# Causal linear attention and an ELU feed-forward on one core: the state term moved to 64x64 array tiles, w_in loaded in halves, and a new opening order

## The chip, the core and the metric

The kernel runs on one core of a Trainium2 chip. A core has a matrix engine (TensorE, PE in the profile, with its weight loads as PEld), a vector engine (VectorE, DVE), an activation engine (ScalarE, ACT), a general engine (GpSimd, POOL) and a queue engine (SyncE, SP). The metric is the device time of one execution in microseconds (us); a time quoted for a kernel is the median of its runs.

## The reference

`q`, `k`, `v` are 4 batches x 8 heads x 768 positions x 64, float32. Attention is linear and causal with a decay `lam[h]` per head; in blocks,

```python
intra = (qb @ kb.T) * Dmask          # Dmask[i, j] = lam ** (i - j) for i >= j, else 0
out   = intra @ vb + (qb * lam ** (pos + 1)) @ kv_state
kv_state = lam ** block * kv_state + (kb * lam ** (block - 1 - pos)).T @ vb
```

The attention's output is laid out as `x` of 3072 tokens x 512 (8 heads of 64 side by side), and goes through a feed-forward: `h = x @ w_in` (512 x 2048), `g = h` where positive and `exp(h) - 1` elsewhere, `out = g @ w_out` (2048 x 512), float32.

## The kernel before

The work is cut into 24 chunks g of 128 positions. Chunk g is block g // 4 of batch g % 4, so four consecutive chunks are the four batches at one place of the sequence. All matrix work is in float16 with float32 sums. Chunks 0 to 3 are treated one by one, the others in pairs. `T`, `S`, `P`, `U`, `1` and `2` below are the letters by which the kernel's own list names the steps:

- `T` (L284) transposes q and k of a chunk on PE with an identity, for chunks 0 to 7. VectorE multiplies q^T by `qs`, the powers of lam, and ScalarE copies k^T. For chunks 8 and up SP does it with two transposing DMAs (L274, in the step `W`).
- `S` (L305) makes the scores. Two heads share the 128 rows of a transposed block, so each matmul has 64 rows; the two heads of a block of rows go to two PSUM banks. VectorE multiplies the scores by the mask (`pp`, L330).
- `P` (L339) makes x^T of a chunk in one bank: per pair of heads two matmuls with v (L350, 128 rows x 64 columns of the array), and from chunk 4 on two with the state (L356). There the state of a pair of heads is a 128x128 matrix whose off-diagonal 64x64 blocks are zero, zeroed once at the start by VectorE and ScalarE (`z`, `Z`), and half of it is the weights of a 128x64 matmul. One instruction per chunk takes the bank to SBUF as `xt`: for chunks 0 to 7 a copy on ScalarE or VectorE, after that a multiplication by `qs` on VectorE.
- `U` (L401) makes the chunk's contribution to the state, and VectorE adds it (L431), in two instructions of 64 rows, to the old state times lam^128, which POOL has made in two instructions of 64 rows (L390). POOL also makes `kd`, k times powers of lam (L192).
- `1:g:j` (L491) is the first GEMM for a quarter (a single chunk) or an eighth (a pair) of the 2048 columns, one PSUM bank of 512 values; a third number halves it. ScalarE takes the exponential and the positive part, VectorE combines them to `g` (L480). `2:g:j` (L532) is the second GEMM's part; after the last part ScalarE copies the result out and SP stores it.

The order on every engine is the order in which this program issues instructions; nothing is moved afterwards. `OPEN` (L52) lists the steps up to chunk 10's, written out by hand; behind it a loop (L643) adds the rest, in which a pair's scores are followed at once by a burst `B:` with the U and P steps of the previous pair. `w3` is three matmuls on zeros, which fill a wait on PE. `BANKS` (L67) gives PSUM banks to steps: A to D, M0, M1, and H, which has two buffers.

All of q, k, v, w_in and w_out come in by DMAs that POOL issues, with a cast to float16, in the order of `POOL_ORDER` (L47): `k0` is k of chunk 0, `i0` a slice of 256 columns of w_in, `o0` one of 256 rows of w_out, `d2` the product kd of chunk 2, `m4` the state product of chunk 4. Chunk 0's q alone is issued by SP (`raw_q`). These DMAs take eight semaphores in turn, so that each waits on POOL until the eighth before it has landed.

Of the kernel before, what the change touches and what calls it, by code (L numbers as in the profile page):

```python
# [14 lines left out]
def kernel(  # L15
# [23 lines left out]
    GPE = 8  # L39
# [8 lines left out]
        "k0 k1 q1 v0 q2 i1 k2 i0 v1 v2 i2 i3 o0 q3 k3 d2 d0 o1 i4 o2 i5 v3 o3 o5 o4 i6 i7 q4 o7 d1 o6 "  # L48
        "k4 m4 v4 k6 q6 v6 q10 m5 d4 k8 d5 d3 k10 d6 m6 q8 v10 d7 m7 v8"
# [18 lines left out]
        "S0=M0,D S1=A,C S2=B,C S3=D,B P0=M1 P1=M1 P2=M0 P3=D U0=M0 U1=D U2=B U3=M1 T0=B,A T1=B,M1 "  # L68
        "T2=B,M1 T3=A T4=B T5=D T6=A T7=M1 M2=C M3=M0 H0_2=A H3_0=B X2=1 H0_1=C H1_3=A X3=1 X7=1 X4=1 "
        "H2_1=D X0=1 H1_1=M0"  # L70
# [26 lines left out]
    for i in range(7):  # L97
# [23 lines left out]
        [cpool.tile([128, NHP, 128], FP16, name=f"st{b}_{i}") for i in range(2)]  # L121
# [49 lines left out]
    def emit_wi(i):  # L171
        f0 = sum(WI[:i]) * 128
        nc.gpsimd.dma_start(  # L173
            out=wi16[i][:],
            in_=moe_w_in[:, f0 : f0 + WI[i] * 128].rearrange("(k p) f -> p k f", p=128),
        )
# [37 lines left out]
    def zero_st1(b):  # L214
        nc.vector.memset(st[b][1][:], 0.0)


# [8 lines left out]
    qs = cpool.tile([128, NHP, 128], FP32, name="qs")  # L226
    ks = cpool.tile([128, H], FP32, name="ks")
# [77 lines left out]
    def att_S(g):  # L305
        qt, kt = qkT[g]
        psS[g] = [
            bank(f"S{g}", hh, [128, NHP, 128], FP32, f"psS{g}_{hh}") for hh in range(2)
        ]
        for hp in range(NHP):  # L310
            for hh in range(2):
                r = slice(hh * 64, (hh + 1) * 64)
                nc.tensor.matmul(  # L313
                    psS[g][hh][:, hp, :], lhsT=kt[r, hp, :], rhs=qt[r, hp, :],
                    start=True, stop=True,
                )
# [21 lines left out]

    def att_P(g):  # L339
        cb, b = divmod(g, B)  # L340
        until(E_done, g)
        if cb > 0:
            until(Y_done, g - B)
        vt = of(vg, g)
        qt, _ = qkT[g]
        po = bank(f"P{g}", 0, [128, NHP, 128], FP32, f"psO{g}")
        R = [slice(0, 64), slice(64, 128)]
        for hp in range(NHP):
            for hh, r in enumerate(R):
                nc.tensor.matmul(  # L350
                    po[r, hp, :], lhsT=vt[:, 2 * hp + hh, :], rhs=Pt[(g, hh)][:, hp, :],
                    start=True, stop=(cb == 0), skip_group_check=True,
                )
            if cb > 0:
                for r in R:
                    nc.tensor.matmul(  # L356
                        po[r, hp, :], lhsT=st[b][cb % 2][:, hp, r], rhs=qt[:, hp, :],
                        start=False, stop=True, skip_group_check=True,
                    )

        def evacuate():
            g0 = GFIRST[g]
            n = GSIZE[g0]
            if g0 not in xg:
                xg[g0] = asb.tile(
                    [128, NHP, n * 128], FP16, tag=f"xt{n}", name=f"xt{g0}",
                    bufs=4 if n == 1 else 2,
                )
            dst = xg[g0][:, :, (g - g0) * 128 : (g - g0 + 1) * 128]
            if g < GPE:  # L370
                (nc.vector.tensor_copy if f"X{g}" in TAGS else nc.scalar.copy)(dst, po[:])
            else:
                nc.vector.tensor_tensor(out=dst, in0=po[:], in1=qs[:], op=ALU.mult)  # L373
            X_done.add(g)

        return [evacuate]

    stt = {}

    def att_M(g):  # L380
        cb, b = divmod(g, B)
        if cb == NCB - 1:
            return
        assert f"U{g - B}" in seen
        until(Y_done, g - B)
        old = st[b][cb % 2]
        for hh in range(2):
            r = slice(hh * 64, (hh + 1) * 64)
            tmp = asb.tile([128, NHP, 64], FP32, tag="stt", name=f"stt{g}_{hh}", bufs=8)
            nc.gpsimd.tensor_tensor(  # L390
                out=tmp[r], in0=old[r, :, r],
                in1=upp[r].unsqueeze(2).broadcast_to([64, NHP, 64]), op=ALU.mult,
            )
            stt[(g, hh)] = tmp
# [6 lines left out]
    def att_U(g, pu=None):  # L401

        cb, b = divmod(g, B)
        if cb == NCB - 1:
            return []
        vt = of(vg, g)
        if pu is None:
            full = bank(f"U{g}", 0, [128, NHP, 128], FP32, f"psU{g}")
            for hp in range(NHP):
                nc.tensor.matmul(  # L410
                    full[:, hp, :].rearrange("p (h e) -> p h e", h=2),
                    lhsT=kds[g][:, 2 * hp : 2 * hp + 2, :],
                    rhs=vt[:, 2 * hp : 2 * hp + 2, :], start=True, stop=True,
                )
        else:
            for hp in range(NHP):
                for hh in range(2):
                    r = slice(hh * 64, (hh + 1) * 64)
                    nc.tensor.matmul(  # L419
                        pu[r, hp, :], lhsT=kds[g][:, 2 * hp + hh, :], rhs=vt[:, 2 * hp + hh, :],  # L420
                        start=True, stop=True, skip_group_check=True,
                    )
        new = st[b][(cb + 1) % 2]

        def update(hh):
            r = slice(hh * 64, (hh + 1) * 64)
            src = full[r, :, r] if pu is None else pu[r, :, :]
            if cb == 0:
                nc.vector.tensor_copy(new[r, :, r], src)
            else:  # L430
                nc.vector.tensor_tensor(  # L431
                    out=new[r, :, r], in0=stt.pop((g, hh))[r], in1=src, op=ALU.add
                )
            if hh == 1:
                Y_done.add(g)

        return [lambda: update(0), lambda: update(1)]

    def burst(*ops):
# [3 lines left out]
        for o in ops:  # L443
            if o[0] == "P":
                evs += att_P(int(o[1:]))
# [130 lines left out]
    def zero_st(b):  # L576
        nc.scalar.memzero(st[b][0][:])

# [18 lines left out]
    def ready(t):  # L597

        g = int(t[1:])
        if t[0] == "P":  # L600
            assert g < B or f"U{g - B}" in seen
        if t[0] == "U" and g < 2 * B:
            assert "c2" in seen
            assert f"{'z' if g < B else 'Z'}{g % B}" in seen
# [4 lines left out]
    def run(t):  # L609
# [7 lines left out]
        if w in "PUzZ":  # L617
            ready(t)
        if w == "S":
            for g in a:  # L620
                att_S(g)
# [10 lines left out]
        else:  # L632
            {"T": att_T_pe, "1": mm1, "2": mm2, "Z": zero_st, "z": zero_st1,
             "q": lambda g, e: cast_raw(g, "q", e), "k": lambda g, e: cast_raw(g, "k", e),
             "c": const, "W": pool_work, "L": load_pair,
             "M": next_M, "w": zero_matmuls}[w](*a)
# [28 lines left out]
    for t in prog:  # L665
        run(t)
# [34 lines left out]
```

## Time and profile before

| | |
|---|---|
| median of 3 runs | 211.45 us (211.43 to 211.71) |
| profiled execution | 211.74 us, of which the instructions span 210.0 us |
| PE busy | 204.5 us, 97% of the span, 2075 matmuls |
| DVE, ACT, POOL busy | 137.3, 125.3 and 98.9 us |
| first GEMM (L511), second GEMM (L541) | 98.6 and 96.8 us of PE's busy time |
| matmuls with v (L350), with the state (L356) | 192 and 160 |
| granted PE clock | 1.00 |

The span runs from the first to the last instruction. Matmuls overlap in the array, so the busy time of a group is the time in which at least one of its matmuls was under way; the chain of waits, which gives each piece the time up to the next start, tells better what a group costs. Its columns are start in us, length in us, and the work.

### The profile page before, as it was taken

The numbers are of one execution on the slowest core, as the hardware profiler recorded it, in microseconds if no ns is written. First come the engines' busy times: TensorE is split into PE (matmuls) and PEld (weight loads), VectorE is DVE, ScalarE is ACT, GpSimd is POOL, SyncE is SP. The second block draws the span as 40 slices with busy tenths as digits, with TensorE's granted clock in tenths as the row PEclk, the third lists the DMA queues.
The fourth block names the chain that finished last, engine by engine and source line by source line (L and its number), as shares of the span: only waits on it lengthen the run. The fifth ranks groups of instructions, "written<-read, shape, count | busy, mean of one in ns | idle before, by whom it ended". The sixth has DMA issues, their size and how long they took to land.

```text
span 210.0 us, 5117 instructions
## 1 busy us (share of the span) xinstructions
PE 204.5 (97%) x2075; PEld 140.3 (67%) x2075; DVE 137.3 (65%) x238; ACT 125.3 (60%) x241; POOL 98.9 (47%) x113
## 2 busy tenths in 40 slices
PE   7899999999999999999999999999999999999994
PEld 3458767767777766767667667666666667666653
DVE  6778843699847879678686787676676763433320
ACT  2728565765675866586377377377377477577640
POOL 8999789699935948259294379100000000000000
PEclk9999999999999999999999999999999999999999
DMA  8999999999999999997999929993520110110112
GB/s 105 161 180 187 194 201 188 155 181 154 96 110 210 118 200 143 178 117 47 167 140 113 165 77 106 184 148 69 128 75 0 53 50 0 53 52 16 37 50 100
DMA packets 103079, 24.71 MB, mean 118 GB/s; under 512 B 93200, under 2 KB 100624, under 8 KB 103056
## 3 DMA queue, kind: packets, MB, share of 16 engines
q0 software_dynamic: 79760, 13.50, 85.0%
q1 hardware_dynamic: 22768, 10.76, 26.2%
q8 instruction: 16, 0.26, 0.5%
q10 hardware_dynamic: 528, 0.13, 0.3%
q14 instruction: 7, 0.06, 0.1%
HBM read 27.40 MB, written 6.29 MB: 160 GB/s over the span
## 4 chain that ended last, share of the span: by engine, by line
PE 80%; POOL 9%; DMA 9%; issue 1%; DVE 0%; POOLq 0%
PE psM L541 36%; PE psH L511 34%; DMA wo<-in_moe_w_out_dram 9%; PE psS L313 3%; PE psO L350 2%; PE psO L356 2%; POOL qn L133 2%; POOL wi L173 2%; POOL kn L133 2%; POOL kd L192 1%; POOL vn L133 1%; PE psU L419 1%; POOL wo L180 1%; PE psT L294 1%; PE psMrest L553 0%
## 5 line engine op out<-in xcount | busy, mean ns | idle before, releaser
L511 PE MATMUL psH<-xt,wi 128*128 128x256 f16 (+1 forms) x896 | 98.6, 257 | 0.1
L541 PE MATMUL psM<-wo,g 128*128 128x512 f16 (+1 forms) x384 | 96.8, 377 | 0.2
L520 ACT ACTIVATE e<-psH 128x512 f32<-128x512 f32 x96 | 57.4, 598 | 63.8 <-PE psH L511 63.4
L511 PEld LDWEIGHTS <-wi 128*128 128x128 f16 x896 | 78.0, 98 | 24.7
L480 DVE SCALAR_TENSOR_TENSOR g<-e,r 128x512 f16<-128x512 f32 x64 | 46.8, 732 | 40.6 <-ACT r L527 40.1
L541 PEld LDWEIGHTS <-g 128*128 128x128 f16 x384 | 35.8, 98 | 26.8 <-issue 0.4
L527 ACT ACTIVATE r<-psH 128x512 f32<-128x512 f32 x64 | 38.1, 595 | 0.0
L330 DVE TENSOR_TENSOR pp<-psS,mask 128x512 f16<-128x512 f32 x48 | 30.9, 684 | 1.9 <-PE psS L313 1.8
L480 DVE SCALAR_TENSOR_TENSOR g<-e,psH 128x512 f16<-128x512 f32 x32 | 21.9, 685 | 14.0 <-ACT psH L527 13.8
L192 POOL TENSOR_TENSOR kd<-kn,ks 128x512 f16<-128x512 f16 x20 | 21.5, 1081 | 16.7 <-DMA kn<-in_k_dram 15.9
L390 POOL TENSOR_TENSOR stt<-st,upp 64x256 f32<-64x256 f16 x32 | 21.6, 674 | 13.1 <-DVE st L431 11.7
L527 ACT ACTIVATE psH<-psH 128x512 f32<-128x512 f32 x32 | 19.1, 598 | 0.0
L567 ACT COPY osb<-psM 128x512 f32<-128x512 f32 (+1 forms) x24 | 14.1, 589 | 6.4 <-PE psM L541 6.4
L133 POOL DMA_DIRECT2D kn<-in_k_dram x14 | 15.5, 1111 | 1.3 <-POOLq L685 0.8
L133 POOL DMA_DIRECT2D vn<-in_v_dram x14 | 15.4, 1109 | 0.0
L133 POOL DMA_DIRECT2D qn<-in_q_dram x13 | 14.7, 1129 | 0.5 <-DMA wo<-in_moe_w_out_dram 0.5
L431 DVE TENSOR_TENSOR st<-stt,psU 64x256 f16<-64x256 f32 x32 | 13.3, 416 | 0.7
L350 PE MATMUL psO<-pp,vn 128*64 128x128 f16 x192 | 12.3, 221 | 0.3 <-ACT kT L302 0.2
L373 DVE TENSOR_TENSOR xt<-psO,qs 128x512 f16<-128x512 f32 x16 | 10.5, 685 | 2.4 <-PE psO L356 2.3
L350 PEld LDWEIGHTS <-vn 128*64 128x64 f16 x192 | 10.1, 109 | 2.8 <-issue 2.3
L88 PE MATMUL psZ<-zero 128*128 128x512 f16 x26 | 9.1, 514 | 1.2 <-DVE zero L83 1.2
L356 PE MATMUL psO<-qT,st 128*64 128x128 f16 x160 | 10.1, 219 | 0.0
(49 smaller groups left out, 91.6 us busy)
## 6 DMA issues: line engine op xcount, KB each, us to landing
out_dram<-osb SPq DMA_DIRECT2D x19, 256.0 KB, 3.6
qn<-in_q_dram POOLq DMA_DIRECT2D x10, 256.0 KB, 7.2
kn<-in_k_dram POOLq DMA_DIRECT2D x10, 256.0 KB, 9.3
vn<-in_v_dram POOLq DMA_DIRECT2D x10, 256.0 KB, 8.4
wi<-in_moe_w_in_dram POOLq DMA_DIRECT2D x8, 256.0 KB, 6.7
wo<-in_moe_w_out_dram POOLq DMA_DIRECT2D x8, 256.0 KB, 8.8
out_dram<-osb SPq DMA_DIRECT2D x8, 128.0 KB, 1.8
kn<-in_k_dram POOLq DMA_DIRECT2D x4, 128.0 KB, 5.1
```

Of the source, the lines that this page charges most:

```text
L133: nc.gpsimd.dma_start(out=t[:].rearrange("p b h d -> p (b h) d"), in_=src)
L192: nc.gpsimd.tensor_tensor(out=kd[:], in0=of(kg, g), in1=ks[:].unsqueeze(2).broadcast_to([128, H, 64]), op=ALU.mult,)
L330: nc.vector.tensor_tensor(out=P[:], in0=pts[hh][:], in1=mask[:, hh::2, :], op=ALU.mult)
L350: nc.tensor.matmul(po[r, hp, :], lhsT=vt[:, 2 * hp + hh, :], rhs=Pt[(g, hh)][:, hp, :], start=True, stop=(cb == 0), skip_group_check=True,)
L356: nc.tensor.matmul(po[r, hp, :], lhsT=st[b][cb % 2][:, hp, r], rhs=qt[:, hp, :], start=False, stop=True, skip_group_check=True,)
L390: nc.gpsimd.tensor_tensor(out=tmp[r], in0=old[r, :, r], in1=upp[r].unsqueeze(2).broadcast_to([64, NHP, 64]), op=ALU.mult,)
L480: nc.vector.scalar_tensor_tensor(out=flat, in0=e[:], scalar=-1.0, in1=r[:], op0=ALU.add, op1=ALU.min)
L511: nc.tensor.matmul(pH[:, f * n * 128 : (f + 1) * n * 128], lhsT=wi16[i][:, kk, w * 128 : (w + 1) * 128], rhs=xg[g0][:, kk, :], start=(kk = ...
L520: nc.scalar.activation(e[:], pH[:], AF.Exp)
L527: nc.scalar.activation(r[:], pH[:], AF.Relu)
L541: nc.tensor.matmul(psM[g][:, cols], lhsT=gts[(g, j * FB + f)], rhs=wo16[i][:, w, cols], start=mm2_done[g] == 1, stop=mm2_done[g] == NFT, s ...
L567: eng.copy(o[:], src)
```

## The change

Five things change together.

1. **x^T's rows.** A block of 128 rows of x^T now holds heads k and 4+k instead of 2k and 2k+1. The rows of w_in have to follow, so a slice of w_in is loaded by two transfers, each to 64 partitions: rows 0 to 255 of w_in and rows 256 to 511.
2. **The state term.** The state is kept as 64 columns per pair of heads, without the zero blocks, and its matmuls are 64 rows x 64 columns of the array. The two heads of a pair lie on different rows and write different banks, heads of the two halves lie on different columns; so four matmuls in a row use four different quarters of the array. A pair of chunks is done together (`att_PP`): the state term of both first, then the matmuls with v into the same two banks, each of which holds two blocks of rows for both chunks. Two instructions per pair take the banks out; from chunk 8 on VectorE multiplies by `qx`, the powers of lam in the new order of heads, which ScalarE makes at the step `x`. All evacuations of chunks 0 to 7 are on ScalarE.
3. **The state's update.** `U` of a single chunk is eight matmuls of 128x64 instead of four of 128x128 (as it was in the bursts already). VectorE's update and POOL's product are one instruction of 128 rows each instead of two of 64, and nothing is zeroed.
4. **Scores just ahead of a burst** (S14:15 to S22:23) are made in 64x64 tiles too, 32 matmuls instead of 16.
5. **Order.** `POOL_ORDER`, `OPEN` and `BANKS` are new: the opening transposes chunk 1 before chunk 0, makes the scores of both in a row, and starts the first GEMM after P1; chunks 8 to 11 come in another order.

```diff
-        "k0 k1 q1 v0 q2 i1 k2 i0 v1 v2 i2 i3 o0 q3 k3 d2 d0 o1 i4 o2 i5 v3 o3 o5 o4 i6 i7 q4 o7 d1 o6 "
-        "k4 m4 v4 k6 q6 v6 q10 m5 d4 k8 d5 d3 k10 d6 m6 q8 v10 d7 m7 v8"
+        "k0 q1 k1 q2 v0 i1 v1 k2 i0 v2 i2 i3 o0 q3 k3 d2 o1 d0 i4 o2 i5 v3 o3 o5 d1 i6 i7 o4 o7 m4 o6 "
+        "q4 k4 k6 d3 v4 q6 k8 v6 d4 d6 q10 d7 d5 m5 v8 q8 v10 m7 k10 m6"
...
-        "z0 q0:2 c1 c0 w2 w3 c3 Z1 c2 T0 Z3 T1 S0 w3 w3 P0 w5 S1 T2 1:0:0:0 P1 z1 S2 Z2 1:1:0:0 "
-        "1:1:0:1 P2 1:0:0:1 1:0:1:0 1:0:1:1 z2 1:2:1:0 1:2:0:0 1:2:0:1 U0 2:0:0:0 1:2:1:1 T3 1:1:1:0 "
...
-        "W11 W10 1:6:4 B:P8:P9:U8:U9 1:6:5 1:6:6 2:6:0 2:6:1 L12 1:6:7 2:6:2 1:8:0 S10:11 2:6:3 1:8:1 "
+        "c1 c0 q0:1 w5 c3 T1 T0 w2 S0 S1 w3 P0 c2 w2 T2 P1 1:0:0:0 1:1:0:0 S2 1:1:0:1 P2 1:0:0:1 "
+        "1:0:1:0 1:2:0:0 1:0:1:1 1:2:0:1 1:2:1:0 U0 2:0:0:0 1:2:1:1 T3 1:1:1:0 1:1:1:1 2:1:0:0 "
+        "2:0:0:1 2:2:0:1 S3 1:1:2:0 1:0:2:0 2:2:0:0 2:2:1:0 2:0:1:0 1:2:2:0 1:0:2:1 1:2:2:1 P3 M "
+        "2:1:1:0 U1 2:1:1:1 2:0:1:1 1:1:2:1 1:3:2:0 2:0:2:1 1:3:2:1 2:1:0:1 1:3:0:0 2:2:1:1 1:1:3:0 "
+        "1:0:3:0 1:2:3:0 1:2:3:1 2:0:2:0 1:1:3:1 2:1:2:0 2:2:2:1 2:2:2:0 1:3:0:1 2:1:2:1 2:2:3:1 "
...
+        "B:P8:P9:U8:U9 L14 1:6:5 2:6:0 1:6:6 2:6:1 L12 1:8:4 S10:11 W12 1:6:7 2:6:2 1:8:5 W13 2:7:2 "
...
-        "S0=M0,D S1=A,C S2=B,C S3=D,B P0=M1 P1=M1 P2=M0 P3=D U0=M0 U1=D U2=B U3=M1 T0=B,A T1=B,M1 "
+        "S0=M0,B S1=A,D S2=D,C S3=D,B P0=M1 P1=B P2=M1 P3=D U0=M0 U1=B U2=D U3=M1 T0=A,A T1=B,C "
...
-        [cpool.tile([128, NHP, 128], FP16, name=f"st{b}_{i}") for i in range(2)]
+        [cpool.tile([128, NHP, 64], FP16, name=f"st{b}_{i}") for i in range(2)]
...
-        nc.gpsimd.dma_start(
-            out=wi16[i][:],
-            in_=moe_w_in[:, f0 : f0 + WI[i] * 128].rearrange("(k p) f -> p k f", p=128),
-        )
+        for c in range(2):
+            nc.gpsimd.dma_start(
+                out=wi16[i][c * 64 : (c + 1) * 64],
+                in_=moe_w_in[c * 256 : (c + 1) * 256, f0 : f0 + WI[i] * 128].rearrange(
+                    "(k p) f -> p k f", p=64
+                ),
+            )
...
+    def emit_qx():
+        for c in range(2):
+            r = slice(c * 64, (c + 1) * 64)
+            nc.vector.tensor_copy(loglam_x[r, :], loglam[r, c * NHP : (c + 1) * NHP])
+        for k in range(NHP):
+            nc.scalar.activation(
+                qx[:, k, :], row[:], AF.Exp, scale=loglam_x[:, k : k + 1]
+            )
...
-    def att_S(g):
+    def att_S(g, split):
...
+        keys = [slice(0, 64), slice(64, 128)] if split else [slice(0, 128)]
...
+                for m in keys:
+                    nc.tensor.matmul(
+                        psS[g][hh][m, hp, :], lhsT=kt[r, hp, m], rhs=qt[r, hp, :],
+                        start=True, stop=True,
+                    )
...
+        for s in range(2):
+            for hh in range(2):
+                for hp in (s, s + 2):
+                    nc.tensor.matmul(
+                        po[R[hp // 2], 2 * s + hh, :], lhsT=vt[:, 2 * hp + hh, :],
+                        rhs=Pt[(g, hh)][:, hp, :], start=True, stop=True, skip_group_check=True,
+                    )
...
+    def att_PP(g0):
+        pos2 = [
+            bank(f"P{g0 + hh}", 0, [128, 2, 2, 128], FP32, f"psO{g0}_{hh}") for hh in range(2)
+        ]
+        for c in range(2):
+            g = g0 + c
+            cb, b = divmod(g, B)
             until(Y_done, g - B)
...
+            qt, _ = qkT[g]
+            for s in range(2):
+                for hp in (s, s + 2):
+                    for hh in range(2):
+                        nc.tensor.matmul(
+                            pos2[hh][R[hp // 2], s, c, :], lhsT=st[b][cb % 2][R[hh], hp, :],
+                            rhs=qt[R[hh], hp, :], start=c == 0 and s == 0, stop=False,
+                            skip_group_check=True,
+                        )
...
+        def evacuate(hh):
+            dst, src = x_of(g0)[:, hh::2, :], pos2[hh][:].rearrange("p s c t -> p s (c t)")
+            if g0 < GPE:
+                nc.scalar.copy(out=dst, in_=src)
...
+        tmp = asb.tile([128, NHP, 64], FP32, tag="stt", name=f"stt{g}", bufs=4)
+        nc.gpsimd.tensor_tensor(
+            out=tmp[:], in0=st[b][cb % 2][:],
+            in1=upp[:].unsqueeze(2).broadcast_to([128, NHP, 64]), op=ALU.mult,
+        )
...
         for o in ops:
+            if o[0] == "P" and int(o[1:]) >= B and int(o[1:]) % 2 == 0:
+                evs, values = att_PP(int(o[1:]))
+        for o in ops:
...
-    for t in prog:
-        run(t)
+    for t, following in zip(prog, prog[1:] + [""]):
+        run(t, split=following[:2] == "B:")
```

More of the change, by code (lines that the diff above doesn't have):

```diff
@@ L337, in att_E, with x_of @@
         return [lambda: half(0), lambda: half(1)]
+    R = [slice(0, 64), slice(64, 128)]
+    def x_of(g):
+        g0 = GFIRST[g]
+        n = GSIZE[g0]
+        if g0 not in xg:
+            xg[g0] = asb.tile(
+                [128, NHP, n * 128], FP16, tag=f"xt{n}", name=f"xt{g0}",
+                bufs=4 if n == 1 else 2,
+            )
+        return xg[g0]
     def att_P(g):
-        cb, b = divmod(g, B)
         until(E_done, g)
-        if cb > 0:
-            until(Y_done, g - B)
         vt = of(vg, g)
-        qt, _ = qkT[g]
@@ L385, in att_M @@
         until(Y_done, g - B)
[L386 to L394, printed above, removed]
+        tmp = asb.tile([128, NHP, 64], FP32, tag="stt", name=f"stt{g}", bufs=4)
+        nc.gpsimd.tensor_tensor(
+            out=tmp[:], in0=st[b][cb % 2][:],
+            in1=upp[:].unsqueeze(2).broadcast_to([128, NHP, 64]), op=ALU.mult,
+        )
+        stt[g] = tmp
     def next_M():
@@ L407, in att_U, with update @@
         if pu is None:
-            full = bank(f"U{g}", 0, [128, NHP, 128], FP32, f"psU{g}")
-            for hp in range(NHP):
+            pu = bank(f"U{g}", 0, [128, NHP, 64], FP32, f"psU{g}")
+        for hp in range(NHP):
+            for hh in range(2):
                 nc.tensor.matmul(
-                    full[:, hp, :].rearrange("p (h e) -> p h e", h=2),
-                    lhsT=kds[g][:, 2 * hp : 2 * hp + 2, :],
-                    rhs=vt[:, 2 * hp : 2 * hp + 2, :], start=True, stop=True,
-                )
[L415 to L422, printed above, removed]
+                    pu[R[hh], hp, :], lhsT=kds[g][:, 2 * hp + hh, :], rhs=vt[:, 2 * hp + hh, :],
+                    start=True, stop=True, skip_group_check=True,
+                )
         new = st[b][(cb + 1) % 2]
-        def update(hh):
-            r = slice(hh * 64, (hh + 1) * 64)
-            src = full[r, :, r] if pu is None else pu[r, :, :]
+        def update():
             if cb == 0:
-                nc.vector.tensor_copy(new[r, :, r], src)
+                nc.vector.tensor_copy(new[:], pu[:])
             else:
[L431 to L437, printed above, removed]
+                nc.vector.tensor_tensor(out=new[:], in0=stt.pop(g)[:], in1=pu[:], op=ALU.add)
+            Y_done.add(g)
+        return [update]
     def burst(*ops):
@@ L607, in ready, with run @@
         seen.add(t)
-    def run(t):
+    def run(t, split=False):
         w, *a = t[0], *t[1:].replace(":", " ").split()
@@ L616, in run @@
         a = [int(x) for x in a]
-        if w in "PUzZ":
+        if w in "PU":
             ready(t)
@@ L620, in run @@
             for g in a:
-                att_S(g)
+                att_S(g, split)
             for g in a:
```

70 lines of the change are left out of this document (31 added, 39 removed), and 17 rows, old and new, of tables (BANKS, OPEN).

## The prediction

> **What bounds the kernel now.** I read the page's engine rows and chain first, then the busy time of three stretches, then the chain piece by piece, then the first 20 us instruction by instruction.
>
> ```profile
> span 210.0 us, 5117 instructions
> PE 204.5 (97%) x2075; PEld 140.3 (67%) x2075; DVE 137.3 (65%) x238; ACT 125.3 (60%) x241; POOL 98.9 (47%) x113
> PE 80%; POOL 9%; DMA 9%; issue 1%; DVE 0%; POOLq 0%
> ```
> ```profile
> 19.68:38.80 19.12, 18.95 (x225) 13.54 (x223) 11.41 (x21) 11.45 (x23) 16.61 (x20) 1.00 1.61 190
> ```
>
> The columns of the stretch are length, then busy time of PE, PEld, DVE, ACT, POOL, then granted clock. From 19.68 us on, TensorE (PE) is never idle for long: the order written for it is carried out as fast as it streams. So two things count: when PE reaches a given point of its order, and how many microseconds of streaming lie behind it. I cut at the first state matmul, U0, because before it both kernels do the same blocks (T0-T2, S0-S2, P0-P2 and nine first-GEMM half-blocks).
>
> ```profile
> 19.68 0.39 PE L410 MATMUL psU<-vn,kd 128*128 128x128 f16 x4
> ```
> ```profile
> 28.16 10.62 DMA wo<-in_moe_w_out_dram
> 38.82 0.59 PE psM L541 x2
> ...
> 46.07 0.22 PE psU L410 x4
> ...
> 47.74 0.25 PE psU L419 x16
> ...
> 115.92 0.86 PE psM L541 x4
> 116.78 0.55 PE psS L313 x16
> 117.33 0.37 PE psU L419 x16
> 117.70 0.06 PE psO L350 x2
> 117.76 0.06 PE psO L356 x2
> ...
> 118.60 0.97 PE psM L541 x4
> ...
> 132.69 0.55 PE psS L313 x16
> ...
> 207.15 0.29 DVE osb L565
> ```
>
> From U0 to the last copy PE takes 207.15 - 19.68 = 187.47 us.
>
> **The streaming behind U0.** In the chain, two psO matmuls side by side take 0.06 us, 27.9 ns each (32 of them fill 117.70 to 118.60). A change of the array's shape costs a little: sixteen psS in pairs would take 0.45 us at that rate and take 0.55; psU takes 0.37 right behind psS and 0.25 behind psO (47.74); four psM take 0.97 behind psO, else 0.86. So one change costs 0.11 us (0.10 to 0.12).
>
> ```profile
> L356 PE MATMUL psO<-qT,st 128*64 128x128 f16 x160 | 10.1, 219 | 0.0
> ```
>
> - State term: 160 matmuls of 128x64, two at once, are 160 x 27.9 ns = 4.46 us. As 64x64 tiles they are again 160, four at once if each streams as before: 2.23 us, a gain of 2.23. No row shows four at once. Bounds: no overlap beyond two, gain 0; or the spacing of psU (0.25 / 16 = 15.6 ns each), gain 1.96. I take 2.23, since psO and psS pairs stream at their full rate.
> - Scores just ahead of a burst become 32 matmuls of 64x64 instead of 16 of 64x128, for S14:15 to S22:23. Four at once they cost the same 0.45 us (bounds 0 and, two at a time, +0.45 each, 2.2 together; at psU's spacing +0.05 each).
> - U0 to U3: 4 x 0.22 us become 4 x 8 matmuls at 15.6 ns, 0.50: a gain of 0.38.
> - Shape changes: U0 to U3 were full 128x128 matmuls among their like and now switch in and out, +8. Bursts 4, 6, 8, 10 and 22 have no scores directly ahead and switch once more (64x64, then 128x64), +5. In bursts 12 to 20 the split scores and the state term share one shape: no change. 13 x 0.11 = +1.43 (1.3 to 1.6).
>
> Sum behind U0: -2.23 - 0.38 + 1.43 = **-1.2 us** (-0.5 to -1.3, and +3.3 if four never overlap).
>
> **The opening.** These rows carry it; "third transfer in POOL's queue" is q1 before and k1 after.
>
> ```profile
> 3.13 0.88 POOL L133 DMA_DIRECT2D qn<-in_q_dram  x1
> 7.37 0.30 ACT L256 ACTIVATE ks<-loglam,pos 128x8 f32<-128x8 f32 x1
> 7.58 0.19 ACT L257 ACTIVATE upp<-loglam_p 128x4 f32<-128x4 f32 x1
> 8.09 1.83 POOL L133 DMA_DIRECT2D vn<-in_v_dram  x2
> 8.24 0.10 PEld L294 LDWEIGHTS <-qn 128*128 128x128 f16 x1 [0.37 <-DMA qn<-in_q_dram]
> 8.68 0.38 PE L294 MATMUL psT<-ident,qn 128*128 128x128 f16 x4 [0.64 <-DVE qT L301]
> 9.10 0.69 DVE L301 TENSOR_TENSOR qT<-psT,qs 128x512 f16<-128x512 f16 x1 [0.47 <-PE psT L294]
> 9.32 0.59 ACT L302 COPY kT<-psT 128x512 f16<-128x512 f16 x1 [0.34 <-PE psT L294]
> 9.83 1.58 POOL L173 DMA_DIRECT2D wi<-in_moe_w_in_dram  x2
> 13.33 0.61 PE L511 MATMUL psH<-xt,wi 128*128 128x128 f16 x8
> 14.92 0.40 PE L313 MATMUL psS<-qT,kT 64*128 64x128 f16 x8 [0.21 <-DVE qT L301]
> 15.34 1.29 DVE L330 TENSOR_TENSOR pp<-psS,mask 128x512 f16<-128x512 f32 x2 [0.20 <-PE psS L313]
> 16.46 0.60 ACT L520 ACTIVATE e<-psH 128x512 f32<-128x512 f32 x1 [0.82 <-PE psH L511]
> 16.96 0.59 ACT L527 ACTIVATE psH<-psH 128x512 f32<-128x512 f32 x1
> 16.99 2.85 PE L511 MATMUL psH<-xt,wi 128*128 128x128 f16 x48
> 17.10 0.69 DVE L371 CAST xt<-psO 128x512 f16<-128x512 f32 x1 [0.47 <-PE psO L350]
> 20.29 2.14 POOL L180 DMA_DIRECT2D wo<-in_moe_w_out_dram  x3 [0.41 <-DMA wo<-in_moe_w_out_dram]
> ```
> ```profile
> L192 POOL TENSOR_TENSOR kd<-kn,ks 128x512 f16<-128x512 f16 x20 | 21.5, 1081 | 16.7 <-DMA kn<-in_k_dram 15.9
> ```
>
> POOL issues a load of q, k or v for one chunk in 0.87 us (8.09 to 9.83 is two), a w_in slice in 0.75 (two in 1.58, the last of which shows 0.84), a w_out slice in 0.70 (three in 2.14). Half a w_in slice has a w_out slice's number of runs (64 x 4 = 128 x 2), so I price it 0.70: 8 x (2 x 0.70 - 0.75) = +5.2 us on POOL in all. The second half of slice 0 is now the eleventh issue. The third starts at 3.13 as before (PE sees it land at 8.24); then q2 4.00, v0 4.87, i1 5.74 and 6.44, v1 7.14, k2 8.01, i0 8.88 and 9.58. The same slice before:
>
> ```profile
> L173 POOL DMA_DIRECT2D wi<-in_moe_w_in_dram x1: 812/812/812, 7.3 to 7.3; - x1
> ...
> DMA to landing us min/median/max: 5.5/5.5/5.5
> ```
>
> So i0 lands at 12.9 before and about 15.0 (9.58 + 5.5) after, and before's first half-block starts at 13.33. Now the new order, step by step: T1 comes first and ends when k1 lands, 8.24 + 0.2. T0's two halves share bank A, one buffer, so k0 is transposed only when DVE has read q0: qT0 8.88 to 9.57 (0.42 behind PE, as 8.68 to 9.10), k0 at 9.63, kT0 by the same 0.42 on ACT 10.05 to 10.64. S0 10.70, S1 10.95. DVE then makes four pp in a row, 0.42 behind S0 and 0.64 each: 11.12 to 13.7. P1 ends 13.9. ACT's queue is ks (behind a small DVE step, 13.9), upp (+0.21), kT2 (+0.2), xt1 (+0.50, the spacing of 16.46 and 16.96): xt1 14.8 to 15.4. PE: block 1:0:0:0 at 15.0, 1:1:0:0 at 15.45, S2 at 16.0, pp2 16.42 to 17.7, and only one half-block (0.45) stands between S2 and P2, so P2 ends at 17.9 after about 1.2 us of waiting; xt2 (0.47 behind) 18.2 to 18.8. Six half-blocks (16.99 to 19.68 before, 2.69) from 17.95, U0 at 20.75. The opening is **+1.1 us** (bounds: 0, if P2's wait is covered, to +2).
>
> Off the path: the sixteen 64-partition state updates on DVE and products on POOL that halve in number, and the zeroing that goes, free DVE, ACT and POOL time that nothing waits for. qx adds four 128x128 exponentials to ACT at chunk 4, while ACT has 40% idle; 0 as long as mm1's banks come free in time, otherwise up to 1.3 us. Two evacuations per pair stay two.
>
> **What is late next.** The order behind U0 meets the loads: i4's second half is issued, by the spacings above (v2, i2, i3, o0, q3, k3, kd2 1.08, o1, kd0 1.08, i4), at about 20 and lands near 25; PE gets to 1:1:2:0 at 20.75 + 4.2 = 24.95. w_out slice 4 lands near 34.5 and is wanted near 35.7. So the loads just hold. One wait goes: w_out slice 6 ended a 0.3 us stall at 38.82; it is now queued ahead of q4 and wanted 1.1 us later: **-0.3**.
>
> **Sum**: 210.0 + 1.1 - 1.2 - 0.3 = 209.6 us of span. The profiled execution took 211.74 with 1.74 outside the span; the median of the runs is 211.45, 0.29 lower. So 211.45 - 0.4 = **211.0 us**; own range 210.2 to 211.8. A measurement of this kernel tells about 0.2%, 0.42 us, from no change.
>
> **Rivals.**
> - *The opening is not later (211.0 - 1.1 = 209.9).* If waits in T0 and P2 overlap better than my walk has it, U0 stays near 19.7 and the saved streaming shows whole. For: P1 is through before the first half-block now, where before the 3.66 us from 13.33 to 16.99 held three half-blocks (1.34), P1, S2 and P2 (0.22 each) and six shape changes (0.66): 1.0 us was waiting. Against: kT0, the four pp and xt1 stand in a row.
> - *The loads fall behind PE (slower, about 212.5).* W_out slice 4, the third of the issues at 20.29, left POOL at 21.7 before; now, behind all sixteen halves, it leaves near 28.8 (20 + seven halves and o2, o3, o5 at 0.70, v3 0.87, kd1 1.08). It decides from the point where landing takes over 6.9 us from issue (35.7 - 28.8). For: the page's median for w_out is 8.8 us, and slice 6 took 10.6. Against: those stood in a backed-up queue, and here the issue itself is the brake. Landing in 8.4 us gives +1.5.
>
> ```profile
> wo<-in_moe_w_out_dram POOLq DMA_DIRECT2D x8, 256.0 KB, 8.8
> ```
>
> - *Four tiles do not overlap (about 215.4).* The state term keeps its 4.46 us (+2.2) and the split scores double (+2.2). Against: psS overlaps two row halves and psO two column halves, both at full rate. The Trainium skill, "TensorE: Matmul & The Clock Gate", Part 1 (the passage on 56 against 53.3 ns), states that starts never come closer than about 25 ns. By that floor 160 state matmuls would take 4.0 us and the 160 split scores 4.0 instead of 2.23: 214.5. The trace does not agree for tiles: psU runs at 15.6 ns each.
> - *Half-slices write no faster than whole ones (about 218).* The two slices issued at 9.83 landed 1.3 us apart:
>
> ```profile
> DMA to landing us min/median/max: 6.1/6.4/6.7
> ```
>
>   (0.74 apart in issue, 0.6 more in landing.) Were each half to take 1.3 us, the loads before w_out slice 6 would take 10.4 us longer and PE would wait for some 7. The Trainium skill, "SBUF — State Buffer", section on Door 1, the DMA port swizzle, says bandwidth goes by the ports that the partitions reach, and 64 neighbouring ones reach half of the sixteen. No run here shows such a transfer. Against: two halves go to different ports and are in flight together.
>
> **How the numbers follow.** As summed 0.45, opening not later 0.20, loads behind 0.24, tiles 0.06, half-slices 0.05. The first splits about its centre: 0.25 faster, 0.17 same, 0.03 slower; the second is faster; the rest slower. Faster 0.45, same 0.17, slower 0.38. The range is 209.7 to 213.0: it takes in the second case and most of the third, and leaves out the last two and a tail.
>
> **What would show it.** First half-block near 15.0, U0 near 20.75, P2's second half waiting for DVE. A late pair's period, 116.78 to 132.69, is 15.9 us and should become 15.7. The state pieces in the chain at 0.11 us per chunk, split psS unchanged at about 0.55. No wait at w_out slice 6; short ones, if any, at w_in slice 4 and w_out slice 4. Wrong if U0 is off by over 0.7 us, if psO of the state shows pairs of 28 ns, or if PE shows waits of over 0.5 us between 20 and 45 us.

## The result and the profile after

The changed kernel takes 210.88 us (median of 21 runs, 210.36 to 211.88), the kernel before 211.45 in the runs beside it (211.26 to 211.86). The ratio is 0.9972, 95% interval 0.9961 to 0.9983: 0.28% faster, 0.6 us, where 211.0 was predicted. Its times spread 1.5 us, against 0.6 before; that was not foreseen, and the experiments follow it up. (In later sets of runs the kernel before has single times up to 213.36 too, but half of its times stay within 0.4 us, and half of the changed kernel's within 0.6 or more.)

The profiled execution took 210.94 us. The page after:

```profile
span 209.2 us, 5248 instructions
PE 202.2 (97%) x2167; PEld 137.5 (66%) x2167; DVE 124.4 (59%) x210; ACT 128.3 (61%) x246; POOL 91.8 (44%) x105
PE 91%; POOL 4%; DMA 3%; DVE 1%; issue 0%; POOLq 0%
```

The chain of waits after (start, length, work), first the opening, then a late pair's burst:

```profile
9.34 5.32 DMA wi<-in_moe_w_in_dram
...
14.74 1.05 PE psH L553 x16
15.79 0.38 PE psS L325 x8
16.17 0.57 DVE pp L342
...
17.50 0.36 PE psO L372 x6
17.86 2.79 PE psH L553 x48
20.65 0.25 PE psU L459 x8
...
116.89 0.57 PE psS L325 x32
117.47 0.27 PE psO L395 x16
117.73 0.37 PE psU L459 x16
118.11 0.45 PE psO L409 x16
118.55 0.97 PE psM L583 x4
...
132.55 0.57 PE psS L325 x32
```

And the instructions in order of time, with what ended the idle time before them:

```profile
9.18 0.38 PE L304 MATMUL psT<-ident,kn 128*128 128x128 f16 x4 [1.01 <-DVE qT L311]
...
13.35 0.40 PE L304 MATMUL psT<-ident,kn 128*128 128x128 f16 x4 [0.21 <-DMA kn<-in_k_dram]
...
14.74 1.05 PE L553 MATMUL psH<-xt,wi 128*128 128x128 f16 x16 [0.65 <-DMA wi<-in_moe_w_in_dram]
...
17.50 0.36 PE L372 MATMUL psO<-pp,vn 128*64 128x128 f16 x6 [0.35 <-DVE pp L342]
...
20.58 0.32 PE L459 MATMUL psU<-vn,kd 128*64 128x64 f16 x8
...
206.37 0.29 DVE L607 COPY osb<-psMrest 128x128 f32<-128x128 f32 x1 [5.14 <-PE psMrest L595]
```

U0 starts at 20.58 instead of 19.68: the opening costs 0.90 more. From U0 to the last copy it is 206.37 - 20.58 = 185.79 instead of 187.47: 1.68 less. Together the span is 0.8 shorter. The state term of a pair is one piece of 0.27 us for 16 matmuls, where 16 matmuls in pairs of 0.06 (eight rows of the chain of before) took 0.45. That is so where split scores stand right ahead of it; behind a GEMM, in the other five pairs, the piece is 0.35 with its change of shape. The last load for which PE waits is slice 0 of w_in, at 14.65; no load holds it up behind U0.

### The profile page after: what moved, and what is told of

Its sections match the earlier page's. It is cut to its first block, busy times and chain, and to the rows that moved or that the text cites. A ratio compares the mean times of both kernels' runs of the same rounds, so it can differ in the third digit from the quotient of the medians.

```text
span 209.2 us, 5248 instructions
## 1 busy us (share of the span) xinstructions
PE 202.2 (97%) x2167; PEld 137.5 (66%) x2167; DVE 124.4 (59%) x210; ACT 128.3 (61%) x246; POOL 91.8 (44%) x105
## 4 chain that ended last, share of the span: by engine, by line
PE 91%; POOL 4%; DMA 3%; DVE 1%; issue 0%; POOLq 0%
PE psH L553 41%; PE psM L583 40%; PE psS L325 3%; DMA wi<-in_moe_w_in_dram 3%; PE psO L409 2%; PE psU L459 2%; PE psO L395 1%; POOL kn L133 1%; PE psT L304 1%; POOL wi L174 1%; POOL qn L133 1%; POOL vn L133 1%; DVE pp L342 1%; PE psMrest L595 0%; PE psO L372 0%
## 5 line engine op out<-in xcount | busy, mean ns | idle before, releaser
L439 POOL TENSOR_TENSOR stt<-st,upp 128x256 f32<-128x256 f16 x16 | 11.7, 730 | 11.9 <-DVE st L469 11.9
L420 DVE TENSOR_TENSOR xt<-psO,qx 128x512 f16<-128x512 f32 x16 | 10.5, 686 | 4.1 <-PE psO L409 4.1
L174 POOL DMA_DIRECT2D wi<-in_moe_w_in_dram x16 | 10.3, 685 | 0.0
L88 PE MATMUL psZ<-zero 128*128 128x512 f16 x22 | 8.3, 534 | 1.2 <-DVE zero L83 1.2
L325 PEld LDWEIGHTS <-kT 64*64 64x64 f16 (+1 forms) x272 | 5.5, 101 | 4.6 <-issue 3.0
L325 PE MATMUL psS<-qT,kT 64*64 64x128 f16 (+1 forms) x272 | 7.8, 218 | 0.2 <-ACT kT L312 0.2
L311 DVE TENSOR_TENSOR qT<-psT,qs 128x512 f16<-128x512 f16 x8 | 5.3, 686 | 2.4 <-PE psT L304 2.4
```

What stands on the lines that cost most here:

```text
L174: nc.gpsimd.dma_start(out=wi16[i][c * 64 : (c + 1) * 64], in_=moe_w_in[c * 256 : (c + 1) * 256, f0 : f0 + WI[i] * 128].rearrange("(k p) f ...
L325: nc.tensor.matmul(psS[g][hh][m, hp, :], lhsT=kt[r, hp, m], rhs=qt[r, hp, :], start=True, stop=True,)
L439: nc.gpsimd.tensor_tensor(out=tmp[:], in0=st[b][cb % 2][:], in1=upp[:].unsqueeze(2).broadcast_to([128, NHP, 64]), op=ALU.mult,)
```

## The experiments

All edits are to the changed kernel. The theory at the start: behind U0 the change gains about 1.7 us, and the new opening gives 0.9 of it back by waits of its own (k0's transposes for the shared bank, the first half-block for slice 0, P2 for `pp`). If that is so, mending the opening shortens the whole.

**The shared bank alone.**

```diff
-T0=A,A
+T0=A,M1
```

> Theory (the landing of w_in slice 0 sets the first half-block, and k2 sets T2): k0 is transposed about 1.2 us earlier (near 8.0 us instead of 9.18) and S0 starts 0.6 earlier, but T2 still waits for k2 until 13.3 and the first half-block for slice 0 until 14.65, so U0 stays at 20.6 and the time at 210.9. Rival (the shared bank is on the path): U0 and the time come 0.5 us earlier.

Measured: 210.93 us (210.25 to 212.42). k0's transposes came at 7.98, S0 at 9.09, and U0 at 19.94, but not because of the bank:

```profile
12.25 0.40 PE L304 MATMUL psT<-ident,kn 128*128 128x128 f16 x4 [0.27 <-DMA kn<-in_k_dram]
...
14.10 1.05 PE L553 MATMUL psH<-xt,wi 128*128 128x128 f16 x16 [1.11 <-ACT xt L378]
```

T2 still waited for k2, which landed a microsecond earlier in this execution (12.2 instead of 13.3). The row names xt1 as what ended the wait at 14.10, but xt1 was made by 13.76; the second half of slice 0 landed at 14.01 (14.65 in the changed kernel), and the first half-block starts 0.09 behind that landing in both. Two runs below with the shared bank have U0 at 19.8 and 19.9. The bank is not on the path, as the theory had it; what moved U0 is two landings, of k2 and of slice 0, that differ from one execution to the next.

**Slice 0 ahead of slice 1.**

```diff
-k0 q1 k1 q2 v0 i1 v1 k2 i0 v2
+k0 q1 k1 q2 v0 i0 v1 k2 i1 v2
```

> Slices 0 and 1 change places in POOL's queue. Theory: slice 0 lands near 11.3 and the first half-block starts when P1 is through, near 14.15 instead of 14.74; the second then waits for xt1 (14.86), so S2 starts near 15.35 instead of 15.79 and U0 comes 0.4 earlier: about 210.5, and if this landing makes the times of the changed kernel spread, they spread less than its 1.5 us. Rival (something else behind it, slice 1 or xt, is as late): U0 within 0.15 of 20.58, no gain.

Measured: 210.99 us (210.26 to 211.74). The first half-block came at 13.98 and U0 at 20.01, as the theory had it. The time did not follow, and the spread stayed. The instructions show where the 0.57 us went:

```profile
29.63 1.02 PE L583 MATMUL psM<-wo,g 128*128 128x512 f16 x4 [0.59 <-DMA wo<-in_moe_w_out_dram]
```

PE, being early, waited 0.59 us for w_out slice 3, which landed at 29.6.

**P2 two half-blocks later.**

```diff
-S2 1:1:0:1 P2 1:0:0:1 1:0:1:0 1:2:0:0
+S2 1:1:0:1 1:0:0:1 1:0:1:0 P2 1:2:0:0
```

> P2 stands two half-blocks later. Theory: its wait of 0.85 us for pp2 goes, and U0 comes 0.8 earlier (19.8), less what 1:2:0:0 then waits for xt2 (P2 through near 17.2, xt2 near 18.2, some 0.9 us later, so 0.5 to 0.9 of waiting): a net of 0 to 0.3 us, 210.6 to 210.9. Rival (xt2 is made in time): 210.1.

Measured: 211.09 us (210.79 to 212.76). The wait of P2 went and a longer one took its place:

```profile
18.60 1.95 PE L553 MATMUL psH<-xt,wi 128*128 128x128 f16 x32 [1.45 <-ACT xt L378]
```

U0 came at 20.48, although slice 0 landed early in this execution (13.6). The wait for xt2 was 1.45, not 0.5 to 0.9: this edit alone gains nothing.

**All of the opening.** The three edits, T2 in bank M1, and

```diff
-k0 q1 k1 q2 v0 i1 v1 k2 i0 v2
+k0 q1 k1 v0 i0 v1 q2 k2 i1 v2
...
-T2 P1 1:0:0:0 1:1:0:0 S2 1:1:0:1 P2 1:0:0:1 1:0:1:0 1:2:0:0 1:0:1:1 1:2:0:1
+P1 1:0:0:0 T2 1:1:0:0 1:1:0:1 S2 1:0:0:1 1:0:1:0 P2 1:2:0:0 1:2:0:1 1:0:1:1
```

> All three together, with v0 and slice 0 ahead of q2, P1 and its first half-block ahead of T2, and P2 last. Theory (the opening cost 0.9 us by waits of its own, which lie on loads and copies): first half-block near 12.8, U0 between 18.8 and 19.6, 1.0 to 1.8 us earlier; of this the loads behind take some back (slice 4's second half landed at 23.96 and would be wanted from 23.1 on, so up to 0.9 of waits): time 209.3 to 210.4. Rival (the loads are the brake everywhere): U0 earlier, but the waits behind it grow by the same amount and the time stays at 210.9.

Measured: 211.28 us (210.44 to 212.40); the first half-block at 12.35, 2.4 us earlier. Then:

```profile
16.70 0.61 PE L553 MATMUL psH<-xt,wi 128*128 128x128 f16 x8 [1.50 <-DMA wi<-in_moe_w_in_dram]
...
30.22 1.02 PE L583 MATMUL psM<-wo,g 128*128 128x512 f16 x4 [0.32 <-DMA wo<-in_moe_w_out_dram]
```

U0 came at 20.20, not between 18.8 and 19.6: PE also waited 0.7 us for xt2 behind P2. The rival holds: what the order gains is taken back, by the loads at slice 2 of w_in and again at w_out slice 3, and by xt2. The first theory has fallen. **The second:** the loads are the brake up to about 30 us, and the order ahead of that mostly decides where PE waits. Two questions follow: is it POOL's issuing or the transfers themselves, and is there slack in that queue? The next two answer them.

**One transfer per slice of w_in.**

```diff
-for c in range(2): dma(wi16[i][64c:64c+64], rows 256c to 256c+255, p=64)
+dma(wi16[i], "(k p) f -> p k f", p=128)
```

> A slice of w_in is one transfer again, with rows k and 4+k not regrouped: the rows of w_in no longer answer to those of x^T, so the output is not the reference's; all work and its order are unchanged. Theory (halving the transfers costs POOL about 0.5 us of issue per slice, and loads are the brake up to 32 us): slice 0 lands 1.0 earlier (12.6 to 13.6), w_out slice 3 lands 2.5 to 3 earlier (near 26.5), PE waits for no load after the first half-block, the spread of times narrows to that of the kernel before (0.6 us), the median falls to 210.3. Rival (only the landing of slice 0 matters): the median falls by the 0.3 to 0.6 that the profiled execution lost at slice 0, and the spread stays.

Measured: 210.56 us (210.09 to 210.84). The issue and landing of w_out slice 3, in the changed kernel and in this one:

```profile
L183 POOL DMA_DIRECT2D wo<-in_moe_w_out_dram x1: 761/761/761, 23.0 to 23.0; - x1
...
DMA to landing us min/median/max: 6.3/6.3/6.3
```
```profile
L180 POOL DMA_DIRECT2D wo<-in_moe_w_out_dram x1: 746/746/746, 19.8 to 19.8; - x1
...
DMA to landing us min/median/max: 8.6/8.6/8.6
```

Issued 3.2 us earlier, it landed only 1.0 earlier (28.4 instead of 29.4), not 2.5 to 3, and the second slice in the queue, slice 0, landed at 14.3 instead of 14.65. So most of the issuing that is saved turns into time to landing: the transfers are the main brake. The 1.0 is what issuing costs; the next experiment shows where. Two whole slices issued in a row landed 1.33 us apart in this run, two slices in halves 1.3 to 1.6 apart in the changed kernel: mainly the bytes set it, not the number of transfers. The Trainium skill, "SBUF — State Buffer", section "Can I just issue two DMAs to hit both halves?", says that two transfers to 64 partitions each run one behind the other. The trace agrees that they land in a row; that each is slower for its 64 partitions hardly shows in these 1.3 to 1.6 us. What the second transfer per slice costs in time is not settled by six runs: all six are at most 210.84, as are fifteen of the changed kernel's thirty-three, and the ratio is 0.9955 (0.9938 to 0.9972), so some 0.3 us.

**kd of chunk 2 later on POOL.** The busy time of stretches of the changed kernel (length, then PE, PEld, DVE, ACT, POOL), whose last column is the DMAs' GB/s, and one stretch of the run with one transfer per slice:

```profile
14.00:20.00 6.00, 4.77 (x84) 4.20 (x81) 2.41 (x4) 3.79 (x8) 5.90 (x8) 1.00 1.68 187
20.00:26.00 6.00, 6.00 (x86) 4.50 (x84) 3.99 (x8) 4.54 (x9) 6.00 (x9) 1.00 1.24 164
26.00:32.00 6.00, 6.00 (x74) 4.00 (x72) 2.77 (x5) 3.44 (x7) 5.24 (x9) 1.00 1.46 190
```
```profile
20.00:26.00 6.00, 6.00 (x82) 4.26 (x79) 4.09 (x7) 4.18 (x9) 5.36 (x8) 1.00 1.50 194
```

Between 20 and 26 us less arrives: 164 GB/s here, and 173 to 180 in four other executions with this order of loads, instead of 194. POOL has no idle time there: it issues as fast as it can. Ahead of that it makes kd of chunks 2 and 0, 1.06 us each, between its issues, and the queue runs low: slice 4, issued at 18.9, lands within 4.4 us, slices before it in 5.4 to 5.7. The kernel before has both kd at the same place, and 194 GB/s; so the hole comes from kd and halved slices together, and here POOL's issuing is a brake after all. kd of chunk 2 is not wanted before U2, at 40 us.

```diff
-q3 k3 d2 o1 d0 i4 o2 i5 v3 o3 o5 d1 i6 i7 o4 o7 m4 o6 q4
+q3 k3 o1 d0 i4 o2 i5 v3 o3 o5 d1 i6 i7 o4 o7 m4 o6 d2 q4
```

> The product kd of chunk 2 moves on POOL from ahead of w_out slice 1 to behind w_out slice 6; PE wants it only at 40 us. Theory (from w_out slice 2 to slice 5 the loads land 0.05 to 0.4 us ahead of their use, so any late landing in the first 20 us makes PE wait behind U0): the loads from slice 4 of w_in to slice 5 of w_out land 0.6 to 1.0 earlier; U0 stays where it is; times above 211.2 become rare, median 210.5 to 210.7. Rival (only the opening makes the spread): times as those of the changed kernel, median 210.9, highest over 211.5.

Measured: **210.19 us** (210.10 to 210.41), ratio to the kernel before 0.9941 (0.9926 to 0.9956). The hole is filled (191 GB/s; 192 and 193 in the three other runs with kd late):

```profile
20.00:26.00 6.00, 5.85 (x76) 4.01 (x69) 4.52 (x8) 3.75 (x8) 5.39 (x8) 1.00 1.50 191
26.00:32.00 6.00, 6.00 (x78) 4.20 (x76) 2.21 (x5) 3.77 (x8) 5.99 (x9) 1.00 1.34 200
```

w_out slices 3 and 5 landed 0.6 and 0.9 earlier (slice 3 at 28.8 instead of 29.4); slice 4 of w_in not earlier, against the expectation. U0 was at 19.79 here, since slice 0 landed in 4.4 us instead of 5.3, which this edit does not touch. The times narrowed to 0.3 us. The move of one instruction lowers the ratio by 0.0031, about as much as the whole change did (0.0028), though from five runs.

**Together with the opening.** First the bank, slice 0 first and kd late:

```diff
-T0=A,A
+T0=A,M1
...
-i1 v1 k2 i0 v2 i2 i3 o0 q3 k3 d2 o1 d0
+i0 v1 k2 i1 v2 i2 i3 o0 q3 k3 o1 d0
```

> Own bank for k0, slices 0 and 1 exchanged, and kd of chunk 2 late. Theory (opening and loads bind one after the other, so only both together pay): U0 near 19.9 as with each of the first two edits, and no wait for loads behind it: median 210.2 to 210.5. Rival (the loads are slow whatever POOL does, by the traffic itself): the landings stay, waits of 0.5 to 1 us for w_out slices 2, 3 and 5, median 210.9 to 211.1.

Measured: 210.53 us (210.29 to 210.75), U0 at 19.98, no wait behind it. The landings did move (w_out slice 3 at 28.6), against the rival, but the two opening edits added nothing to the late kd. Then the opening with P1 ahead of T2 and P2 ahead of the half-blocks of slices 2 and 3, the bank and load order of "all of the opening", and kd late:

```diff
-T2 P1 1:0:0:0 1:1:0:0 S2 1:1:0:1 P2 1:0:0:1 1:0:1:0 1:2:0:0 1:0:1:1 1:2:0:1
+P1 1:0:0:0 T2 1:1:0:0 1:1:0:1 S2 1:0:0:1 P2 1:0:1:0 1:0:1:1 1:2:0:0 1:2:0:1
```

> The opening with P1 and its half-block ahead of T2, P2 ahead of the half-blocks of slices 2 and 3, and kd of chunk 2 late. Theory: first half-block near 12.4, U0 near 19.0 to 19.5, waits of at most 0.7 in all for w_in slices 2 and 5: median 209.6 to 210.2. Rival (loads are the brake whatever the order): U0 early and the same time lost behind it, 210.8 or more.

Measured: 210.37 us (209.86 to 212.19; the two highest, 211.94 and 212.19, at a granted clock of 0.99, the others up to 211.27 at 1.00). The first half-block came at 12.35, but PE waited 0.63 us for slice 1, 0.58 for P2 and 0.32 for slice 3, and U0 was at 20.01. The lowest time of all, and a wide spread: no better than the late kd alone.

**The changed kernel once more,** unaltered, beside the three runs that follow.

> The changed kernel unaltered, beside the others, as their measure. Theory (a late landing somewhere in the first 20 us comes at another place in every execution and costs it between 0 and 1.5 us): the times spread over 1 us or more again, lowest near 210.4, median 210.7 to 211.0.

Measured: 211.13 us (210.08 to 212.06), ratio 0.9962 (0.9936 to 0.9987). In this execution slice 0 landed in 4.3 us, U0 came at 20.24, and the chain ran through POOL instead:

```profile
15.96 1.08 POOL kd L195
17.04 0.64 POOL wo L183
17.69 1.07 POOL kd L195
18.76 1.11 POOL wi L174 x2
19.87 6.20 DMA wo<-in_moe_w_out_dram
...
26.11 1.02 PE psM L583 x4
```

Both kd stand in the chain that sets the end, by way of w_out slice 2, which lands just as PE gets to it. In the profiled executions of the changed kernel and of all edits to it, w_out slice 3 (issue plus time to landing) landed between 28.4 and 30.2, and the span was 208.5 to 209.8; the span less that landing is always 179.6 to 180.4:

| | slice 3 landed | span | rest |
|---|---|---|---|
| changed kernel, and once more | 29.4, 29.4 | 209.2, 209.4 | 179.8, 180.0 |
| bank; slice 0 first; P2 later; all | 28.5, 29.6, 29.0, 30.2 | 208.5, 209.6, 209.0, 209.8 | 180.0, 180.0, 180.0, 179.6 |
| one transfer; kd late | 28.4, 28.8 | 208.8, 208.6 | 180.4, 179.8 |
| bank, slice 0, kd; opening, kd | 28.6, 28.4 | 208.5, 208.6 | 179.9, 180.2 |
| whole scores; state order; kd, columns | 29.3, 29.5, 29.7 | 209.6, 209.1, 209.3 | 180.3, 179.6, 179.6 |

PE waited visibly for it in four of these only. In the others something ahead of it had held PE up already, an earlier load of the same queue in most, xt2 in "P2 later". So the column tells how far the queue has got; it does not show one cause.

**The scores whole again.**

```diff
-run(t, split=following[:2] == "B:")
+run(t)
```

> Scores ahead of a burst as 16 matmuls of 64x128 again. Theory (the split ones take 0.57 us, the whole ones 0.55, and a change of the array's shape 0.11): five bursts take 0.09 us more each, a late pair 15.75 instead of 15.66, the whole 0.45 us more: 211.3. Rival (the split gives nothing): 15.66 or less, no change.

```profile
117.12 0.55 PE psS L325 x16
117.67 0.35 PE psO L395 x16
...
132.84 0.55 PE psS L325 x16
```

A pair takes 132.84 - 117.12 = 15.72, against 15.66: 0.06 more, in the direction of the theory and two thirds of its size, 0.3 us over five pairs. The median, 211.00 (210.52 to 211.58), cannot tell that from 211.13 beside it.

**The state's matmuls in another order.**

```diff
-for s in range(2): for hp in (s, s + 2): for hh in range(2): state matmul
+for hh in range(2): for s in range(2): for hp in (s, s + 2): state matmul
```

> The state term's matmuls in an order in which only two quarters of the array are used at a time: first all of the heads on rows 0 to 63, then those on rows 64 to 127, the same matmuls. Theory (four at once is what pays): the sixteen of a pair take 0.45 us instead of 0.27, ten pairs 1.8 us more, a late pair 15.85: about 212.7. Rival (matmuls in the same half start behind each other at the same distance anyway): 0.27, no change.

Measured: 0.26 us for sixteen, a pair 132.54 - 116.89 = 15.65; median 210.91 (210.25 to 211.81). The expectation of 0.45 failed, the rival's 0.27 holds. The state's matmuls under way in stretches of 0.055 us (no record ends before the last one, so the count is of all starts so far), with the changed order:

```profile
117.29:117.34 0.06, 0.05 (x4) 1.00 1.55 121
117.34:117.40 0.06, 0.06 (x8) 1.00 1.64 75
117.40:117.45 0.06, 0.06 (x12) 1.00 3.39 52
117.45:117.52 0.07, 0.07 (x16) 1.00 0.66 32
```

Four more start in every 0.055 us, though four in a row in the list now use only two quarters. So the edit did not bring about what it was meant to, and that four at once is what pays is not tested by it. The records show why. In the list, the first matmul into each of the two banks waits until ScalarE is done with it: the first and the fifth here, the first and the second in the changed kernel. In this run's trace it is the first and the third to start that carry such a wait, 13 to 17 ns apart, in all six pairs whose records show both. So the fifth of the list starts third: a matmul whose quarter is free starts ahead of two that stand before it in the list and use a quarter still at work.

The direct evidence for four at once is the starts themselves. Behind a GEMM, in the changed kernel, the first four state matmuls start within 10 ns; in steady flow four start in 56 ns, where psO pairs start two in 56.

**Late kd, and the state in the order of the scores.**

```diff
-q3 k3 d2 o1 d0
+q3 k3 o1 d0
...
-for s in range(2): for hp in (s, s + 2): for hh in range(2): state matmul
+for s in range(2): for hh in range(2): for hp in (s, s + 2): state matmul
```

> kd of chunk 2 late on POOL as in the run with that alone, and the state's matmuls in the order of the split scores (columns change first, then rows). Theory of the late kd: U0 near 19.8, no waits for loads of more than 0.3, median 210.2, spread under 0.6. On the order of the state term: if the uneven starts (16.5 ns each on average instead of 13.9) come from the order, the sixteen of a pair take 0.23 instead of 0.27 and the median is 209.8; if they come from the writes of sums or from the weights, 0.27 and 210.2.

Measured: 210.30 us (210.09 to 211.12), ratio 0.9939 (0.9918 to 0.9960); the sixteen take 0.26. The order does not matter to the time. In the profiled execution PE waited 0.54 us for w_out slice 3, which took 8.1 us to land: a late kd makes such waits rarer, it does not end them. Of the fourteen times of the two kernels that differ from the changed one by a late kd (and this order), twelve are at most 210.43; of the changed kernel's thirty-three, seven.

## Why the prediction came out right

- **Median.** 211.0 predicted, 210.88 measured; faster, as the likeliest case had it. That it came this close is partly luck: terms were off in opposite directions.
- **Opening, +1.1.** Measured +0.90. The walk held in its order: k0 after qT0, four `pp` in a row, xt1, P2's second half behind `pp`, where PE is idle again. First half-block 14.74 (15.0), P2's second half 17.50 (17.7), U0 20.58 (20.75). The times up to S0 came 0.45 earlier (k0 at 9.18, not 9.63): the third transfer, k1, landed at 7.48, while the walk took the 8.24 of q1 before. A mis-sized term: half a slice issues in 0.62 us, not 0.70 (two in 1.25, from the chain, below), so slice 0 landed at 14.65 instead of 15.0.

```profile
5.77 1.25 POOL wi L174 x2
```

  What the step missed is that slice 0's 5.3 us were this execution's. In three others with the same opening it took 4.2 to 4.5; there the first half-block starts at 13.75 to 13.9 and U0 comes at 19.8 to 20.2.
- **Behind U0, -1.5.** Measured -1.7. The starts of PE's matmuls in both profiled executions, added up by kind of work, say where:

| behind U0, us | predicted | measured |
|---|---|---|
| five late pairs with split scores | -1.12 | -0.82 |
| the other five pairs, each with one more change of shape | -0.57 | -0.54 |
| U0 to U3 with their changes | +0.50 | +0.42 |
| waits that go | -0.30 | -0.72 |
| small rest | 0 | -0.04 |

- **State term, split scores, shape changes.** The mechanism held. The sixteen start at the full rate of four per 0.056 us, as taken, but in a late pair their piece is 0.04 longer than four such groups, and the split scores take 0.57 instead of 0.55: 0.06 less gain than predicted, five times. In the other pairs the gain of 0.22 less a change of 0.11 was right (0.10 to 0.14). U0 to U3 take 0.24 to 0.25 instead of 0.22 and bring their changes of about 0.1, as summed; the change into U0 stands ahead of the cut.
- **The late pair, 15.9 to 15.7.** It came to 15.66, but the 15.91 it was read from held a wait of 0.10. The other late pairs of the kernel before take 15.82 (100.96 to 116.78), so the gain is 0.16, not 0.25:

```profile
100.96 0.55 PE psS L313 x16
...
123.91 0.96 PE psM L541 x4
```

- **A wait goes, -0.3.** This is the term that was mis-sized most. The wait for w_out slice 6 was 0.31 and went. Three more of the kernel before went with it: 0.14 in U0's step (0.37 until the next matmul instead of 0.22; w_out slice 0 landed at 20.00), 0.21 ahead of 22.02 (eight matmuls take 0.65 instead of 0.45), and the 0.10 above.

```profile
20.05 0.59 PE L541 MATMUL psM<-wo,g 128*128 128x512 f16 x2
...
21.37 0.61 PE L511 MATMUL psH<-xt,wi 128*128 128x128 f16 x8
22.02 0.60 PE L541 MATMUL psM<-wo,g 128*128 128x512 f16 x2
```
```profile
20.38 0.87 DVE L429 CAST st<-psU 64x256 f16<-64x256 f32 x2
...
122.93 0.87 DVE L431 TENSOR_TENSOR st<-stt,psU 64x256 f16<-64x256 f32 x2
```

  The last two stand right behind VectorE's state updates in halves of 64 rows: the first pair delays the `g` that PE waits for at 22.02, the second ends at 123.80, 0.05 ahead of the next psM. The prediction put the freed VectorE time at nothing, "time that nothing waits for"; by this reading, which no run isolates, 0.3 us hung on it. So the total came out near because a state term put too high and waits put too low cancel, which is luck.
- **"So the loads just hold."** Right to a fault. It was worked out for slice 4 of w_in and slices 4 and 6 of w_out; the tightest one, w_out slice 3, was not. It landed at 29.4, and PE, which reached it at 29.65, had 0.3 us to spare.
- **Rival "the opening is not later" (209.9).** Its U0 near 19.8 did come in several executions, but not its time: the loads take the difference. **Rival "loads fall behind".** The mechanism is right, and the times spread less where it is eased, but it sits at w_out slices 2 and 3, not at slice 4, and costs 0.3 to 0.7 in the edited kernels' executions, not 1.5. Its "here the issue itself is the brake" holds between 20 and 26 us only (164 to 180 GB/s); elsewhere the transfers are, and issue 3.2 us earlier brought 1.0 of landing. Its issue time for slice 4 is a slip, the terms add up to 28.95, not 28.8; measured 27.9.
- **Rival "four tiles do not overlap".** Excluded by 0.27. The floor of about 25 ns between starts, cited there from the Trainium skill, "TensorE: Matmul & The Clock Gate", Part 1, would make it 0.40 by estimate; the trace does not agree for tiles. **Rival "half-slices".** Excluded: two halves take 1.3 to 1.6 us to land, one whole 1.33, not 2.6.

## What to carry to other kernels

When a load queue stands close behind the engine that consumes it, reordering the consumer mostly moves the wait: list for each load when it lands and when it is first used, and look for the smallest difference before shortening anything ahead of it. Then look in the issuing engine's own order for work that is wanted much later and leaves the transfers idle; here one product of 1.06 us, moved back by 14 us, took some 0.7 us off the median and made the long times rarer. And look for PE's small waits in the kernel before, not only the one that ends its chain: four of 0.1 to 0.3 us were worth as much as half the streaming that was saved. A median over many executions, with its spread, said more than any single trace: the profiled execution showed slice 0 as the culprit, others showed w_out.

## What was unexpected of the hardware

- The same order of issues lands differently from one execution to the next: half of slice 0 took 5.3 us in one execution of the changed kernel and 4.3 in another. In the profiled executions the times from issue to landing step up by 0.3 to 1 us at some transfer, at a different one each time, and stay up. What causes the step was not found.
- With a full queue the transfers bring 186 to 200 GB/s between 14 and 32 us (one transfer per slice; two with kd late); issuing earlier then adds to the time to landing. Where POOL issues without a pause and the queue runs low, it is 164 to 180.
- 64x64 tiles: four matmuls start per 0.056 us in three different orders of the list, also where four in a row use only two quarters. Judged by the waits in their records, matmuls then start out of the list's order, the fifth as the third.
